# A 24th of the attention's exponentials as a polynomial on VectorE and GpSimd, and the wide exponential in two parts

## The chip, the cores and the metric

The kernel runs on one core of a Trainium2 chip. The metric is device time in microseconds (us). Before the change the median of three runs is 2979.16 us (2979.04 to 2981.36). Engines are named as the profile names them: PE is TensorE, PEld its weight loads, ACT is ScalarE, DVE is VectorE, POOL is GpSimd, and SP issues most DMAs.

## What is computed

A state-space convolution layer and an attention layer with one key and value head alternate, each twice, on a sequence of 2048 positions by 640 channels. All data is float32. The change touches the attention alone; the reference there, cut to what matters (the layer norm in front and the addition of the input behind are left out):

```
B, S, D = x.shape                    # 1, 2048, 640
H, Dh = 32, 20
q = (x @ wq).reshape(B, S, H, Dh).transpose(0, 2, 1, 3)
k = x @ wk                           # one head of 20 for all 32
v = x @ wv
scores = einsum("bhqd,bkd->bhqk", q, k) * (Dh ** -0.5)
p = softmax(scores)
o = einsum("bhqk,bkd->bhqd", p, v)
return o.transpose(0, 2, 1, 3).reshape(B, S, H * Dh) @ wo
```

The exponentials of the softmax are 32 x 2048 x 2048 in each of the two attention layers. No row maximum is searched in the usual case: a bound is put into two extra rows of the keys, so that the scores are ready for the exponential as they come out of the product.

## The kernel before

The program generates the convolution's kernel, runs convolution layer "a", attention layer "b", convolution layer "c" and attention layer "d". The loop that the change touches is `main_loop`, run once by each attention layer. It goes over 1024 tiles. A tile is 128 keys by 1024 columns: four heads by 256 queries. Its index i counts, from the inside, 16 blocks of keys (t), two halves of a query block (f), eight groups of four heads (hg) and four query blocks (nb). A tile takes three steps:

- `scores(i)` (line 1298): two matrix products into a PSUM tile `sc` of 128 x 1024. PSUM has three buffers of this size (`ps2`), taken in turn, so the scores of a tile wait until the tile three places earlier has been read.
- The exponential. Four tiles of six go the `direct` way: ACT reads `sc` and writes `pt` in SBUF (line 1304). The other two of six, those with i % 6 of 0 and 1, go `aside`: DVE copies `sc` into one half of an SBUF tile `pw` of 128 x 2048 (line 1311), and ACT later takes the exponential of both halves with one instruction of 2048 columns, in place (line 1429).
- `values(i)` (line 1321): four matrix products, one for each head, that add the tile's 128 keys into `po` in PSUM. They read four blocks of 256 columns of `pt` or `pw`.

After 32 tiles `normalize` moves `po` to SBUF and divides by the sums (DVE, lines 1336 to 1352), and SP writes the result into `ot`. `projection` (line 1393) multiplies a piece of `ot` by `wo` and `add` (line 1380, DVE) adds it to `x`. The projections are handed out by a credit, 0.52 for each half of an iteration and at most one per half, so that they lie between the scores and the values.

The order on PE, ACT and DVE is written out by hand (`manual_schedule`). One iteration c stands for six tiles:

```
w = wide.pop(c // 6, None)
if w is not None:
    nc.scalar.activation(flat(w), flat(w), AF.Exp, scale=SCALE)
for h in range(2):
    burst = [(c + 2 + 2 * h, direct), (c + 7 + 5 * h, aside), (c + 3 + 2 * h, direct)]
    for i, put in burst:
        if i < n:
            put(i, scores(i))
    ...
    behind([i for i in range(c - 3 + 3 * h, c + 3 * h) if 0 <= i < n])
```

So ACT runs the wide exponential of tiles c and c + 1, then four direct ones (c + 2 to c + 5). PE runs three scores, three values and perhaps a projection, twice. An aside tile is copied up to two iterations before its wide exponential. There are 171 iterations per layer and 170 wide exponentials. POOL has no arithmetic in the loop: it clears two small tiles, issues loads of weights at iteration 36 (`late_loads`) and a few stores of the result.

Of the kernel before, what the change touches and what calls it, by code (L numbers as in the profile page):

```python
# [11 lines left out]
F32 = mybir.dt.float32  # L12
F32R = mybir.dt.float32r
BF16 = mybir.dt.bfloat16
I32 = mybir.dt.int32
AF = mybir.ActivationFunctionType
ALU = mybir.AluOpType
# [4 lines left out]
P = 128  # L22
# [13 lines left out]
SCALE = 20.0**-0.5  # L36
LIMIT = 32.0 * 20.0**0.5
SAFE = ((LIMIT - 1e-6) / 1.002) ** 2


def channel_order():
# [154 lines left out]
class Net:  # L196
# [894 lines left out]
    def _attn(self, ctx, nm, out):  # L1091
# [19 lines left out]
        with tc.tile_pool(name=f"pj{nm}", bufs=1, reuse_waits="tile") as pj:  # L1111
# [116 lines left out]
            nc.scalar.activation(bnd[:, 1:2], bnd[:, 0:1], AF.Sqrt)  # L1228
            nc.vector.tensor_scalar(flag, bnd[0:1, 0:1], SAFE, None, ALU.is_le)
            nc.vector.tensor_scalar(bnd[:, 3:4], bnd[:, 0:1], SAFE, -1.0, ALU.is_le, ALU.mult)  # L1230

# [30 lines left out]
    def main_loop(self, ap, mp, kt, vt, nm, out):  # L1262
# [10 lines left out]
        tc, nc, qps = self.tc, self.nc, self.qps  # L1273
# [5 lines left out]
        def late_loads(late):  # L1279
            nc.gpsimd.memset(wol, 0.0)  # L1280
            for j in range(4):
                nc.gpsimd.dma_start(wol[32 * j : 32 * j + 20],
                                    self.ins["B_wo"][20 * (28 + j) : 20 * (29 + j)])
            if out is None:
                self.conv_weights(nc.gpsimd, late)

        tiles = [(nb, hg, f, t) for nb in range(4) for hg in range(8) for f in range(2) for t in range(16)]
        pos, pts, ots, wide = {}, {}, {}, {}
        queue, later = [], []

        def scores(i):
            nb, hg, f, t = tiles[i]
            if (nb, hg) not in qps:
                self.load_q(ap, nm, nb, hg)
            sc = self.ps2(f"sc{nm}{i}")
            for par in range(2):
                rows = slice(64 * par, 64 * par + 62)
                nc.tensor.matmul(sc[:, 512 * par : 512 * par + 512], kt[rows, 128 * t : 128 * t + 128],  # L1298
                                 qps[nb, hg][rows, f].rearrange("p a c -> p (a c)"), start=True, stop=True)
            return sc  # L1300

        def direct(i, sc):
            pts[i] = mp.tile([P, 1024], F32, tag="pt", bufs=5, name=f"pt{i}")
            nc.scalar.activation(pts[i], sc, AF.Exp, scale=SCALE)  # L1304

        def aside(i, sc):

            if i // 6 not in wide:
                wide[i // 6] = mp.tile([P, 2, 1024], F32, tag="pw", bufs=3, name=f"pw{i // 6}")
            pts[i] = wide[i // 6][:, i % 6]  # L1310
            nc.vector.tensor_copy(pts[i], sc)  # L1311

        def values(i):
            nb, hg, f, t = tiles[i]
            if (nb, hg) not in pos:
                pos[nb, hg] = self.ps1(f"po{nm}{nb}{hg}", hg % 2)
            po, pt = pos[nb, hg], pts.pop(i)

            for j in range(4):
                c0 = 512 * (j % 2) + 256 * (j // 2)  # L1320
                nc.tensor.matmul(po[32 * j : 32 * j + 32, 256 * f : 256 * f + 256], vt[:, t],  # L1321
                                 pt[:, c0 : c0 + 256], start=(t == 0), stop=(t == 15))

        def chunk(nb, k):
            if (nb, k) not in ots:
# [15 lines left out]
        def flat(a):  # L1341
            return a.rearrange("p a b -> p (a b)")
# [22 lines left out]
        def normalize_last():  # L1365

            po = pos.pop((3, 7))
            inv, steps = inverses(po, "l")
            for call in steps:
                call()  # L1370
            on = mp.tile([P, 512], F32, tag="on", bufs=2, name="onl")
            nc.vector.tensor_tensor(on, po, inv, ALU.mult)
            return on

        def add(nb, u, py, last):

            i, half = u // 2, u % 2
            t = TAUS[4 * nb + i]
            xh = self.x[:, t, 320 * half : 320 * half + 320]
            nc.vector.tensor_tensor(xh, py, xh, ALU.add)  # L1380
            if not last or half == 0:
                return
            if out is None:
                self.stats(t)
            else:
                for jh, eng in enumerate((nc.sync, nc.gpsimd if nb < 3 else nc.scalar)):
                    eng.dma_start(self.rows(out)[jh][:, t], self.x[64 * jh : 64 * jh + 64, t])

        def product(py, o, w, u, m, start, stop, c0=0, n=320):
            i, half = u // 2, u % 2  # L1390
            c0 += 320 * half
            for j in range(0, P, m):
                nc.tensor.matmul(py[j : j + m], o[:, 128 * i + j : 128 * i + j + m], w[:, c0 : c0 + n],  # L1393
                                 start=start, stop=stop)
# [8 lines left out]
        n = len(tiles)  # L1403
        credit, pieces = [0.0], []

        def behind(group):

            for i in group:
                values(i)
                if i % 32 == 31 and i + 1 < n:  # L1410
                    normalize(*tiles[i][:2])
            if not group:
                return
            if group[-1] % 32 >= (15 if group[-1] < n - 32 else 8):
                queue.extend(later)
                later.clear()
            credit[0] = min(credit[0] + 0.52, 1.5)
            if queue and credit[0] >= 1 and group[-1] % 32 not in (0, 1):
                credit[0] -= 1
                projection(tiles[group[-1]][1])  # L1420

        with tc.manual_schedule(engines={mybir.EngineType.PE, mybir.EngineType.Activation,
                                         mybir.EngineType.DVE}):
            for i, put in ((0, direct), (6, aside), (1, direct)):
                put(i, scores(i))
            for c in range(0, n, 6):
                w = wide.pop(c // 6, None)
                if w is not None:
                    nc.scalar.activation(flat(w), flat(w), AF.Exp, scale=SCALE)  # L1429
                for h in range(2):  # L1430
                    burst = [(c + 2 + 2 * h, direct), (c + 7 + 5 * h, aside), (c + 3 + 2 * h, direct)]
                    for i, put in burst:
                        if i < n:
                            put(i, scores(i))
                    if pieces:
                        pieces.pop(0)()
                    if c == 36 and h == 0:
                        late_loads(pts[38])
                    behind([i for i in range(c - 3 + 3 * h, c + 3 * h) if 0 <= i < n])
            behind([n - 1])  # L1440
            on = normalize_last()
            if out is None:
                self.norm("c", 0)

            last = []
            for g in range(3):
                tile_ = self.ps2(f"pl{nm}{g}")
                last += [tile_[:, 0:320], tile_[:, 512:832]]
            last.append(self.ps1(f"pl{nm}6", 0)[:, 0:320])
            last.append(self.ps1(f"pl{nm}7", 1)[:, 0:320])  # L1450
            left = queue + later
            for u in range(8):
                items = [(ots[nb, k], wo[:, k]) for nb, k, v in left if v == u and k < 4]
                items.append((ots[3, 4], wo[:, 4]))
                for n, (o, w) in enumerate(items):
                    product(last[u], o, w, u, P, n == 0, False)
            for u in range(0, 8, 2):
                for v in (u, u + 1):
                    product(last[v], on, wol, v, P, False, True)
                for v in (u, u + 1):  # L1460
                    add(3, v, last[v], True)
# [83 lines left out]
```

## Time and profile before

| What | Value |
|---|---|
| Median of three runs | 2979.16 us |
| The profiled execution: its time, its span | 2978.3 us, 2976.4 us |
| PE busy | 2733.0 us, 92% of the span |
| ACT busy | 2414.1 us, 81% |
| DVE busy | 2027.1 us, 68% |
| POOL busy | 84.9 us, 3% |
| Loop of layer "b", window 735 to 1664 us | ACT 923.66 and PE 908.62 of 929.00 us busy |
| Loop of layer "d", window 2030 to 2957 us | ACT 922.26 and PE 908.94 of 927.00 us busy |
| PE clock granted in both loops | 1.00 |

The page's span runs from the first to the last instruction; what lies outside it is 1.9 us. In the groups of the profile the first number is the busy time of the whole group in us and the second the mean duration of one in ns. Instructions of one engine can overlap in these records (the next starts while the last one writes its end), so on a busy engine the distance from start to start is the price of an instruction, and the duration is what another engine waits for. A row of the timeline merges neighbours of one kind ("x4"): its second number is then from the first start to the last end.

### The profile page before, as it was taken

The numbers are of one execution on the slowest core, as the hardware profiler recorded it, in microseconds if no ns is written. First come the engines' busy times: TensorE is split into PE (matmuls) and PEld (weight loads), VectorE is DVE, ScalarE is ACT, GpSimd is POOL, SyncE is SP. The second block draws the span as 40 slices with busy tenths as digits, with TensorE's granted clock in tenths as the row PEclk, the third lists the DMA queues.
The fourth block names the chain that finished last, engine by engine and source line by source line (L and its number), as shares of the span: only waits on it lengthen the run. The fifth ranks groups of instructions, "written<-read, shape, count | busy, mean of one in ns | idle before, by whom it ended". The sixth has DMA issues, their size and how long they took to land. (4 is left out here: it accounts for less than half of the span.)

```text
span 2976.4 us, 69802 instructions
## 1 busy us (share of the span) xinstructions
PE 2733.0 (92%) x29940; PEld 1570.6 (53%) x29940; DVE 2027.1 (68%) x2486; ACT 2414.1 (81%) x2565; POOL 84.9 (3%) x140
## 2 busy tenths in 40 slices
PE   2776989898999999999999998998999999999999
PEld 0333978775444444444444687774444444444444
DVE  7999899943566666666666699725566656666655
ACT  5888243454999999999999734338999999999997
POOL 0000001100000000000000011000000000000000
PEclk9655999998999999999999999999999999999999
DMA  6114555533200010101010256231001101110100
GB/s 146 34 17 103 183 167 114 139 104 104 82 23 27 22 26 22 28 21 28 23 27 20 88 114 161 65 128 43 22 27 31 35 23 32 35 28 23 44 20 24
DMA packets 144184, 178.81 MB, mean 60 GB/s; under 512 B 59524, under 2 KB 115844, under 8 KB 140244
## 3 DMA queue, kind: packets, MB, share of 16 engines
q1 hardware_dynamic: 119704, 141.90, 16.2%
q0 software_dynamic: 21872, 30.69, 5.6%
q8 instruction: 239, 3.92, 0.6%
q10 hardware_dynamic: 2288, 1.64, 0.2%
q14 instruction: 81, 0.66, 0.1%
HBM read 95.22 MB, written 48.04 MB: 48 GB/s over the span
## 5 line engine op out<-in xcount | busy, mean ns | idle before, releaser
L1304 ACT ACTIVATE pt<-scb 128x1024 f32<-128x1024 f32 x684 | 653.5, 1046 | 14.3 <-PE scb L1298 7.2
L1304 ACT ACTIVATE pt<-scd 128x1024 f32<-128x1024 f32 x684 | 652.5, 1044 | 12.7 <-PE scd L1298 7.2
L1429 ACT ACTIVATE pw<-pw 128x2048 f32<-128x2048 f32 x340 | 657.3, 1933 | 0.0
L1311 DVE COPY pw<-scd 128x1024 f32<-128x1024 f32 x340 | 415.4, 1222 | 218.1 <-PE scd L1298 215.0
L1311 DVE COPY pw<-scb 128x1024 f32<-128x1024 f32 x340 | 414.8, 1220 | 212.4 <-PE scb L1298 206.9
L1298 PE MATMUL scb<-qpb,kt 62*128 62x512 f32 x2048 | 378.6, 449 | 27.1 <-ACT pt L1304 17.7
L1298 PE MATMUL scd<-qpd,kt 62*128 62x512 f32 x2048 | 379.5, 449 | 24.4 <-ACT pt L1304 15.7
L1321 PE MATMUL pob<-pt,vt 128*32 128x256 f32 x5472 | 363.4, 383 | 0.1
L1321 PE MATMUL pod<-pt,vt 128*32 128x256 f32 x5472 | 362.9, 383 | 0.1
L1298 PEld LDWEIGHTS scb<-qpb,kt 62*128 62x128 f32 x2048 | 170.4, 186 | 260.9 <-ACT pt L1304 163.7
L1298 PEld LDWEIGHTS scd<-qpd,kt 62*128 62x128 f32 x2048 | 170.0, 185 | 259.7 <-ACT pt L1304 163.8
L1321 PEld LDWEIGHTS pob<-pt,vt 128*32 128x32 f32 x5472 | 160.6, 110 | 152.0 <-issue 63.9
L1321 PEld LDWEIGHTS pod<-pt,vt 128*32 128x32 f32 x5472 | 160.5, 110 | 152.0 <-issue 63.9
L1321 PE MATMUL pod<-pw,vt 128*32 128x256 f32 x2720 | 182.0, 385 | 1.0 <-DVE x L1380 1.0
L1321 PE MATMUL pob<-pw,vt 128*32 128x256 f32 x2720 | 182.0, 385 | 1.0 <-DVE x L1380 1.0
L1380 DVE TENSOR_TENSOR x<-pyd,x 128x320 f32<-128x320 f32 x149 | 72.6, 487 | 144.0 <-PE pyd L1393 144.0
L1380 DVE TENSOR_TENSOR x<-pyb,x 128x320 f32<-128x320 f32 x149 | 72.7, 488 | 141.0 <-PE pyb L1393 141.0
L1321 PEld LDWEIGHTS pob<-pw,vt 128*32 128x32 f32 x2720 | 71.1, 109 | 74.1 <-issue 42.4
L1321 PEld LDWEIGHTS pod<-pw,vt 128*32 128x32 f32 x2720 | 71.1, 109 | 73.3 <-issue 41.6
L1393 PE MATMUL pyb<-wo,ot 128*32 128x320 f32 x1192 | 107.5, 432 | 0.5 <-DMA ot<-on 0.5
L1393 PE MATMUL pyd<-wo,ot 128*32 128x320 f32 x1192 | 107.5, 432 | 0.4 <-DMA ot<-on 0.4
L654 PE MATMUL zc<-xnc,wf 128*128 128x256 f32 x384 | 87.4, 391 | 4.6 <-ACT xnc L821 4.5
(378 smaller groups left out, 3559.4 us busy)
## 6 DMA issues: line engine op xcount, KB each, us to landing
Akh<-kh SPq DMA_DIRECT2D x10, 2048.0 KB
kh<-Ak SPq DMA_DIRECT2D x5, 2048.0 KB
qhd<-qh SPq DMA_DIRECT2D x40, 256.0 KB
qld<-ql SPq DMA_DIRECT2D x40, 256.0 KB
qpb<-qhd SPq DMA_DIRECT2D x256, 40.0 KB
qpd<-qhd SPq DMA_DIRECT2D x256, 40.0 KB
ot<-on SPq DMA_DIRECT2D x216, 40.0 KB
wi<-in_c_wi SPq DMA_DIRECT2D x16, 512.0 KB
```

The source lines that it names most:

```text
L654: nc.tensor.matmul(zv[:, :, c, kk], self.wf[:, t + 4 * h, j, c, kk], x, start=(n == 0), stop=(n == 3))
L1298: nc.tensor.matmul(sc[:, 512 * par : 512 * par + 512], kt[rows, 128 * t : 128 * t + 128], qps[nb, hg][rows, f].rearrange("p a c -> p (a c) ...
L1304: nc.scalar.activation(pts[i], sc, AF.Exp, scale=SCALE)
L1311: nc.vector.tensor_copy(pts[i], sc)
L1321: nc.tensor.matmul(po[32 * j : 32 * j + 32, 256 * f : 256 * f + 256], vt[:, t], pt[:, c0 : c0 + 256], start=(t == 0), stop=(t == 15))
L1380: nc.vector.tensor_tensor(xh, py, xh, ALU.add)
L1393: nc.tensor.matmul(py[j : j + m], o[:, 128 * i + j : 128 * i + j + m], w[:, c0 : c0 + n], start=start, stop=stop)
L1429: nc.scalar.activation(flat(w), flat(w), AF.Exp, scale=SCALE)
```

## The change

Of the six tiles of an iteration the one with i % 6 = 0 loses its last 256 columns to a polynomial; that is 256 of 6144 columns. DVE copies only 768 columns of it to `pw`, which shrinks to 1792 columns. From the other 256, still in PSUM, DVE makes z, the score times SCALE / ln 2 times 2^23 as a whole number (line 1333 of the changed kernel). The lower 23 bits of z with the exponent of 1.0 give a float `zm` in [1, 2), the upper ones a power of two `ze` (lines 1334 and 1335). The first step of a polynomial of degree 5 in `zm` is made on DVE (1337); then POOL runs four pairs of `tensor_scalar` (multiply and add, line 1340) and `tensor_tensor` (multiply, 1341), the last pair with `ze`. The result `zh` is what `values` reads as fourth block.

The wide exponential is cut into 1280 columns, at its old place, and 512, between the direct exponentials of the first and the second half. `values` takes its blocks in the order 0, 2, 1, 3, so that the 512 columns of the later part are read last. POOL joins the engines whose order is written out.

```
+LOG2 = SCALE / math.log(2.0) * 2.0**23
+LOWEST = -125.0 * math.log(2.0) / SCALE
+POW2 = [0.4982859142799133, 0.35375531624817236, 0.10783493672886799, 0.03864472440553453,
+        -0.00039854327235786966, 0.0018775766733993503]
...
+        def blocks(a):
+            return [a[:, c0 : c0 + 256] for c0 in (0, 512, 256, 768)[: a.shape[1] // 256]]
+
         def direct(i, sc):
-            pts[i] = mp.tile([P, 1024], F32, tag="pt", bufs=5, name=f"pt{i}")
-            nc.scalar.activation(pts[i], sc, AF.Exp, scale=SCALE)
+            pt = mp.tile([P, 1024], F32, tag="pt", bufs=5, name=f"pt{i}")
+            nc.scalar.activation(pt, sc, AF.Exp, scale=SCALE)
+            pts[i] = blocks(pt)

         def aside(i, sc):
-            if i // 6 not in wide:
-                wide[i // 6] = mp.tile([P, 2, 1024], F32, tag="pw", bufs=3, name=f"pw{i // 6}")
-            pts[i] = wide[i // 6][:, i % 6]
-            nc.vector.tensor_copy(pts[i], sc)
+            n, h = i // 6, i % 6
+            if n not in wide:
+                wide[n] = mp.tile([P, 1792], F32, tag="pw", bufs=3, name=f"pw{n}")
+            if h == 1:
+                nc.vector.tensor_copy(wide[n][:, 768:], sc)
+                pts[i] = blocks(wide[n][:, 768:])
+                return
+            nc.vector.tensor_copy(wide[n][:, :768], sc[:, :768])
+            w = wide[n]
+            pts[i] = [w[:, 0:256], w[:, 512:768], w[:, 256:512], power(i, sc[:, 768:])]
+
+        def power(i, sc):
+            z, m, e = (mp.tile([P, 256], I32, tag=t, bufs=b, name=f"{t}{i}")
+                       for t, b in (("z", 1), ("zm", 2), ("ze", 2)))
+            h = mp.tile([P, 256], F32, tag="zh", bufs=3, name=f"zh{i}")
+            c = POW2
+            nc.vector.tensor_scalar(z, sc, LOWEST, LOG2, ALU.max, ALU.mult)
+            nc.vector.tensor_scalar(m, z, 0x7FFFFF, 0x3F800000, ALU.bitwise_and, ALU.bitwise_or)
+            nc.vector.tensor_scalar(e, z, 0x7F800000, 0x40000000, ALU.bitwise_and, ALU.bitwise_xor)
+            m, e = m.bitcast(F32), e.bitcast(F32)
+            nc.vector.scalar_tensor_tensor(h, m, c[4] / c[5], m, op0=ALU.add, op1=ALU.mult)
+            for a, b, f in ((0.5 * c[5], 0.5 * c[3], m), (1.0, 0.5 * c[2], m), (1.0, 0.5 * c[1], m),
+                            (1.0, 0.5 * c[0], e)):
+                nc.gpsimd.tensor_scalar(h, h, a, b, ALU.mult, ALU.add)
+                nc.gpsimd.tensor_tensor(h, h, f, ALU.mult)
+            return h
...
-            for j in range(4):
-                c0 = 512 * (j % 2) + 256 * (j // 2)
-                nc.tensor.matmul(po[32 * j : 32 * j + 32, 256 * f : 256 * f + 256], vt[:, t],
-                                 pt[:, c0 : c0 + 256], start=(t == 0), stop=(t == 15))
+            for j in (0, 2, 1, 3):
+                nc.tensor.matmul(po[32 * j : 32 * j + 32, 256 * f : 256 * f + 256], vt[:, t], pt[j],
+                                 start=(t == 0), stop=(t == 15))
...
         with tc.manual_schedule(engines={mybir.EngineType.PE, mybir.EngineType.Activation,
-                                         mybir.EngineType.DVE}):
+                                         mybir.EngineType.DVE, mybir.EngineType.Pool}):
...
-                if w is not None:
-                    nc.scalar.activation(flat(w), flat(w), AF.Exp, scale=SCALE)
                 for h in range(2):
+                    if w is not None:
+                        cols = w[:, 1280 * h : 1280 + 512 * h]
+                        nc.scalar.activation(cols, cols, AF.Exp, scale=SCALE)
```

What stands on ACT for iteration c = 240 of layer "b", before (`pw40` is its wide tile, `pt242` to `pt245` are its direct ones):

```order
L1429 ACTIVATE pw40_13207<-pw40_13207 128x2048 [waits DVE_49]
L1304 ACTIVATE pt242_13291<-scb242_13288 128x1024 [waits PE_49,Activation_49]
L1304 ACTIVATE pt243_13300<-scb243_13297 128x1024 [waits PE_49,Activation_49]
L1304 ACTIVATE pt244_13323<-scb244_13320 128x1024 [waits PE_49,Activation_49]
L1304 ACTIVATE pt245_13333<-scb245_13330 128x1024 [waits PE_49,Activation_49]
```

and in the changed kernel:

```order
L1461 ACTIVATE pw40_13869<-pw40_13869 128x1280 [waits DVE_49]
L1311 ACTIVATE pt242_13986<-scb242_13983 128x1024 [waits PE_49,Activation_49]
L1311 ACTIVATE pt243_13995<-scb243_13992 128x1024 [waits PE_49,Activation_49]
L1461 ACTIVATE pw40_13869<-pw40_13869 128x512
L1311 ACTIVATE pt244_14019<-scb244_14016 128x1024 [waits PE_49,Activation_49]
L1311 ACTIVATE pt245_14045<-scb245_14042 128x1024 [waits PE_49,Activation_49]
```

ACT has one instruction more and 256 columns fewer, and the second part stands between the two pairs.

On DVE at the same place of layer "b" (tiles 246, 247, 252 and 253 are the aside ones of the next two wide tiles; line 1380 is `add`), before:

```order
L1311 COPY pw41_13268<-scb246_13265 128x1024 [waits PE_49,Activation_49]
L1311 COPY pw41_13268<-scb247_13293 128x1024 [waits PE_49]
L1380 TENSOR_TENSOR x_66<-pyb030_13314,x_66 128x320 [waits PE_49]
L1311 COPY pw42_13328<-scb252_13325 128x1024 [waits PE_49,Activation_49]
L1380 TENSOR_TENSOR x_66<-pyb031_13347,x_66 128x320 [waits PE_49]
L1311 COPY pw42_13328<-scb253_13359 128x1024 [waits PE_49]
```

and in the changed kernel:

```order
L1323 COPY pw41_13947<-scb246_13944 128x768 [waits PE_49,Activation_49]
L1333 TENSOR_SCALAR z246_13949<-scb246_13944 128x256 [waits DVE_49]
L1334 TENSOR_SCALAR zm246_13950<-z246_13949 128x256 [waits DVE_49,Pool_49]
L1335 TENSOR_SCALAR ze246_13951<-z246_13949 128x256 [waits Pool_49]
L1337 SCALAR_TENSOR_TENSOR zh246_13952<-zm246_13950 128x256 [waits DVE_49]
L1320 COPY pw41_13947<-scb247_13988 128x1024 [waits PE_49]
L1410 TENSOR_TENSOR x_66<-pyb030_14009,x_66 128x320 [waits PE_49]
L1323 COPY pw42_14024<-scb252_14021 128x768 [waits PE_49,Activation_49]
L1333 TENSOR_SCALAR z252_14026<-scb252_14021 128x256 [waits DVE_49]
L1334 TENSOR_SCALAR zm252_14027<-z252_14026 128x256 [waits DVE_49,Pool_49]
L1335 TENSOR_SCALAR ze252_14028<-z252_14026 128x256 [waits Pool_49]
L1337 SCALAR_TENSOR_TENSOR zh252_14029<-zm252_14027 128x256 [waits DVE_49]
```

Behind every second aside copy stand four more instructions; the PSUM tile is released after the second of the five.

POOL has nothing at this place before. In the changed kernel one tile's share is:

```order
L1340 TENSOR_SCALAR zh246_13952<-zh246_13952 128x256 [waits DVE_49,PE_49]
L1341 TENSOR_TENSOR zh246_13952<-zh246_13952,zm246_13950 128x256 [waits Pool_49]
L1340 TENSOR_SCALAR zh246_13952<-zh246_13952 128x256 [waits Pool_49]
L1341 TENSOR_TENSOR zh246_13952<-zh246_13952,zm246_13950 128x256 [waits Pool_49]
L1340 TENSOR_SCALAR zh246_13952<-zh246_13952 128x256 [waits Pool_49]
L1341 TENSOR_TENSOR zh246_13952<-zh246_13952,zm246_13950 128x256 [waits Pool_49]
L1340 TENSOR_SCALAR zh246_13952<-zh246_13952 128x256 [waits Pool_49]
L1341 TENSOR_TENSOR zh246_13952<-zh246_13952,ze246_13951 128x256 [waits Pool_49]
```

Each of the eight waits for the one ahead of it to have landed.

More of the change, by code (lines that the diff above doesn't have):

```diff
@@ L1437, in main_loop @@
                     if c == 36 and h == 0:
-                        late_loads(pts[38])
+                        late_loads(pts[38][0])
                     behind([i for i in range(c - 3 + 3 * h, c + 3 * h) if 0 <= i < n])
```

## The prediction, made before the changed kernel had run

> **What bounds the kernel now.** I read the page's busy shares first, then the windows of the two loops, then the timeline of ACT and PE inside one of them. The windows (us of the stretch, then busy us of PE, PEld, DVE, ACT, POOL):
>
> ```profile
> 735.00:1664.00 929.00, 908.62 (x11290) 433.02 (x11294) 575.48 (x673) 923.66 (x843) 5.69 (x17) 1.00 0.10 28
> 2030.00:2957.00 927.00, 908.94 (x11286) 432.55 (x11282) 564.99 (x637) 922.26 (x842) 6.90 (x13) 1.00 0.10 27
> ```
>
> The loops are 1856 of 2976 us. ACT is busy for 99.4% of them and PE for 98%, so busy shares don't tell which one sets the pace; the starts do. The timeline of ACT gives the first and the last wide exponential of each loop, and one iteration between:
>
> ```profile
> 729.26 1.91 ACT L1429 ACTIVATE pw<-pw 128x2048 f32<-128x2048 f32 x1
> 1661.88 1.91 ACT L1429 ACTIVATE pw<-pw 128x2048 f32<-128x2048 f32 x1
> 2024.62 1.91 ACT L1429 ACTIVATE pw<-pw 128x2048 f32<-128x2048 f32 x1
> 2955.74 1.91 ACT L1429 ACTIVATE pw<-pw 128x2048 f32<-128x2048 f32 x1
> ...
> 2030.04 1.94 ACT L1429 ACTIVATE pw<-pw 128x2048 f32<-128x2048 f32 x1
> 2031.84 3.80 ACT L1304 ACTIVATE pt<-scd 128x1024 f32<-128x1024 f32 x4
> 2035.45 1.98 ACT L1429 ACTIVATE pw<-pw 128x2048 f32<-128x2048 f32 x1
> ```
>
> With 169 intervals between the first and the last of 170, an iteration takes 932.62/169 = 5.518 us in layer "b" and 931.12/169 = 5.510 in "d", 5.514 on average. Without a wait ACT needs 1.80 for the wide exponential (2030.04 to 2031.84) and 3.61 for the four direct ones, together 5.41. So ACT sets the pace, and 0.10 us of each iteration are slips.
>
> PE follows closely. Its rows in an iteration with one projection, none of them marked with a wait:
>
> ```profile
> 1011.02 0.97 PE L1298 MATMUL scb<-qpb,kt 62*128 62x512 f32 x6
> 1011.91 1.50 PE L1321 MATMUL pob<-pt,vt 128*32 128x256 f32 x24
> 1013.35 1.07 PE L1298 MATMUL scb<-qpb,kt 62*128 62x512 f32 x6
> 1014.35 1.07 PE L1321 MATMUL pob<-pw,vt 128*32 128x256 f32 x16
> 1015.24 0.61 PE L1321 MATMUL pob<-pt,vt 128*32 128x256 f32 x8
> 1015.67 0.72 PE L1393 MATMUL pyb<-wo,ot 128*32 128x320 f32 x8
> 1016.32 0.97 PE L1298 MATMUL scb<-qpb,kt 62*128 62x512 f32 x6
> ```
>
> From score to score that is 5.30 us. The projection takes 0.65 of it (1015.67 to 1016.32); without one, values to scores take 1.44 (1011.91 to 1013.35) in place of 1.32 (1014.35 to 1015.67), so PE needs 5.30 - 0.65 + 0.12 = 4.77. The rows of DVE below count 298 projections in 342 iterations, 0.87 each: PE's mean is 5.30 - 0.13 x 0.53 = 5.23. **The room between ACT's 5.41 and PE is 0.1 to 0.2 us.**
>
> **The change, ACT.** The wide instruction becomes one of 1280 and one of 512 columns. The price of an SBUF source by size comes from the 1.80 above and from an exponential-sized instruction of 1024 columns elsewhere:
>
> ```profile
> 70.68 1.04 ACT L436 ACTIVATE s<-f 128x1024 f32<-128x1024 f32 x1
> 71.62 1.13 ACT L437 ACTIVATE c<-fa,halfpi 128x1024 f32<-128x1024 f32 x1
> ```
>
> 0.94 from start to start for 1024, 1.80 for 2048: 0.84 ns a column and 0.08 us for the instruction. So 1280 cost 1.16, 512 cost 0.51, together 1.67 in place of 1.80. The 256 columns taken away are worth 0.21, and the second instruction gives 0.08 back. ACT's floor goes from 5.41 to **5.28**.
>
> The place of the second part helps PE. The scores of c + 5 wait for the PSUM tile that the direct exponential of c + 3 reads; the wide part between the pairs puts 0.51 between that release and the time at which ACT wants c + 5. I count on the slips of today going away for that reason, but with PE at 5.30 in most iterations the pace is then PE's: 5.31, and 0.02 more because the projections are not spread evenly (a guess).
>
> **DVE.** Its groups in the loop:
>
> ```profile
> L1311 DVE COPY pw<-scd 128x1024 f32<-128x1024 f32 x340 | 415.4, 1222 | 218.1 <-PE scd L1298 215.0 <-ACT pt L1304 0.2
> L1311 DVE COPY pw<-scb 128x1024 f32<-128x1024 f32 x340 | 414.8, 1220 | 212.4 <-PE scb L1298 206.9 <-ACT pt L1304 1.2
> L1380 DVE TENSOR_TENSOR x<-pyb,x 128x320 f32<-128x320 f32 x149 | 72.7, 488 | 141.0 <-PE pyb L1393 141.0
> L1380 DVE TENSOR_TENSOR x<-pyd,x 128x320 f32<-128x320 f32 x149 | 72.6, 487 | 144.0 <-PE pyd L1393 144.0
> L1336 DVE STREAM_TRANSPOSE tr<-on 128x512 f32<-128x512 f32 x62 | 44.1, 712 | 2.1
> L1352 DVE TENSOR_TENSOR on<-on,tr 128x512 f32<-128x512 f32 x62 | 42.3, 682 | 0.0
> L1347 DVE COPY on<-pod 128x512 f32<-128x512 f32 x31 | 21.3, 689 | 7.9 <-PE pod L1321 6.3 <-DMA qpd<-qhd 1.4 <-DMA qpd<-qld 0.2
> ...
> L117 DVE SCALAR_TENSOR_TENSOR Aa<-B x36: 681/686/693, 407.6 to 566.7; 128x512 f32<-128x512 f32 x36
> L281 DVE TENSOR_SCALAR th<-thr x1: 493/493/493, 10.2 to 10.2; 128x640 f32<-128x640 f32 x1
> ```
>
> A copy out of PSUM takes 0.689 for 512 and 1.22 for 1024 columns: 0.96 for 768 and 0.42 for 256. So the shorter copy saves 0.26, and z costs 0.42. The two bit operations go from SBUF to SBUF; the nearest row, 0.493 for 640 columns, gives 0.29 each (the 0.155 that remain of a copy at no columns, and half its price per column). The first step of the polynomial reads two SBUF operands like L117: 0.42. Together DVE gets -0.26 + 0.42 + 0.29 + 0.29 + 0.42 = 1.16 us more per iteration. It is busy for 575.48 of 929, 62% of 5.51 = 3.42; then 4.58 of 5.33, 86%. What hides this is the time in which DVE waits for scores, 215.0 + 206.9 us or 1.24 per iteration, and for projections, 285 us or 0.84. The PSUM tile is free after copy and z, 1.4 us in place of 1.22, and the next aside scores come 2.6 later. The three instructions behind them stand ahead of the next copy: 1.4 + 1.06 (with the small gaps between) = 2.5 fits in 2.6, with an `add` or a piece of `normalize` (0.49 to 0.71) it doesn't, and the next copy is late. It has about an iteration until its tile is wanted, so most of it is absorbed; I charge 0.05.
>
> **POOL.** The trace has no arithmetic of POOL on more than one element. The nearest rows:
>
> ```profile
> L1280 POOL MEMSET wol<- 128x640 f32 x2 | 1.3, 636 | 233.9 <-PEq L1249 233.9
> L427 POOL MEMSET c<- 128x32 f32 x20 | 3.1, 156 | 187.0 <-DVE e1r L464 141.7 <-DVE resare L261 37.4 <-ACT m L453 7.9
> L592 POOL COPY wf<-pt 1x1 f32<-1x1 f32 x8 | 1.0, 173 | 38.6 <-ACT pt L1304 38.6
> L1527 POOL MEMSET const-float32-0.0<- 128x1 f32 x1 | 0.1, 98 | 0.2 <-issue 0.2
> 598.12 2.79 POOL L1103 MEMSET kt<- 1x1536 f32 x2
> L1103 POOL MEMSET kt<- x4: 1367/1370/1372, 598.1 to 1895.3; 1x1536 f32 x4
> 718.93 2.12 POOL L1282 DMA_DIRECT2D wol<-in_B_wo  x4 [0.30 <-POOL wol L1280]
> 760.56 4.21 POOL L598 DMA_DIRECT2D wf<-in_c_wf  x8
> ```
>
> Writing costs (0.636 - 0.156)/608 = 0.79 ns a column, so 0.33 for 256 columns; reading adds 0.075 at one element (0.173 against 0.098); an instruction that waits for the one ahead on POOL starts 0.05 behind it (two of 1.37 in 2.79). **Low end:** reading is free, eight of 0.33 with eight gaps: 3.1 us. **High end:** every operand is a pass of its own (0.20 each): 0.61 for the `tensor_scalar`, 0.81 for the `tensor_tensor`, chain 6.1. **I take** reading of one operand beside the writing and the second operand as a pass: 0.41 and 0.61, chain 4 x 1.02 + 0.4 = 4.5. The result is wanted two iterations later, so the latency is covered; only the throughput counts, 4.5 of 5.3. The GPSIMD Engine Reference of the Trainium skill (section 3.1) measures 4497 ns for a `tensor_tensor` of 2048 columns and puts one-input operations near line rate; as an estimate that is 0.56 to 0.62 for 256 columns and a chain near 4.3. No run here shows it yet.
>
> Once in layer "b", at iteration 36, clearing and loading the weights (0.64 + 2.12 + 1.00 + 4.21 = 8.0 us of POOL) stand in POOL's order ahead of the polynomial; I charge 1 us.
>
> **The sum.** 5.31 + 0.02 + 0.05 = 5.38 against 5.514, so 0.134 x 340 = 46 us less, 1 us back: 2978.3 (the profiled execution: span 2976.4 and 1.9 around it) - 45 = 2933. The median of the runs is 0.9 above that execution: **2934 us**.
>
> **Rivals.** *POOL's chain sets the pace (slower).* Values of each aside tile with i % 6 = 0 wait for `zh`. It decides from the point at which the eight take over 5.51, 0.63 each with the gap taken off. At the high end, 6.1, the loop is 0.6 x 340 = 204 us longer: 3182. For it speaks that POOL goes from 3% to 85% on operations that no row prices; against it that the MEMSETs lie at half that price.
>
> *POOL and DVE shut each other out.* The two bit operations run at half a price per column, which L281 against a copy shows, and the fourth operation reads two SBUF operands; should DVE use for this a way into SBUF that POOL needs too, then 1.06 us of DVE and the chain can't overlap except in the chain's gaps: 4.5 + 1.06 = 5.56 down to 5.16. With the upper price the loop is 0.05 x 340 = 17 us longer, 2995; in the middle nothing changes, 2980. The Trainium skill's page "SBUF — State Buffer" (section "Who interferes with whom") says just that: such DVE instructions and a POOL instruction hold a shared port pair, and the second to issue blocks fully. The trace of before cannot show it, since POOL was idle in the loop.
>
> *PE keeps the pace near today's.* The slips stay at 0.10 and come on top of PE's 5.30 in most iterations and 5.28 in the rest: 5.45 with the 0.05 of DVE, 22 us less, 2956.
>
> *The split does nothing* because 0.08 per instruction is too low: at 0.21 it would eat the gain. ACT's rows at two sizes exclude that.
>
> **Chances.** The forecast 0.40 (2902 to 2955); PE near today's pace 0.15 (2950 to 2972); POOL and DVE shut out 0.25, of which 0.12 within 0.2% and 0.13 slower (to 3040); POOL's chain 0.20 (2986 to 3182). Faster by over 0.2%, which is about what a measurement of this kernel can tell from no change, 0.55; within it 0.12; slower 0.33. The lower end of the range is ACT's floor without any slip, (5.514 - 5.29) x 340 = 76 us less; the upper end, 3075, takes in the port's case and half of the chain's.
>
> **What would show it.** ACT: starts 1.16 and 0.51 apart behind the two parts; iterations of 5.38 by the first and the last start. DVE: the bit operations at 0.29, and longer ones if POOL shuts them out. POOL: about 4.5 busy per iteration, mean of the two operations near 0.41 and 0.61; PE without waits for `zh`. I am wrong if POOL is busy all the time, if PE waits for POOL or for DVE's copies, or if ACT now waits for scores as long as it has gained.

## The result, and the profile after

| | median, us | range of the runs, us | against before, 95% interval |
|---|---|---|---|
| before | 2980.26 | 2979.04 to 2981.56 (4) | |
| predicted | 2934 | 2902 to 3075 | |
| after | 3004.32 | 3002.54 to 3005.79 (4) | 1.0080 (1.0063 to 1.0098) |

The changed kernel is 24 us slower; 46 us faster was forecast. The first and the last start of the wide exponential's first part, in each of the two loops:

```profile
731.15 1.26 ACT L1461 ACTIVATE pw<-pw 128x1280 f32<-128x1280 f32 x1
1676.10 1.31 ACT L1461 ACTIVATE pw<-pw 128x1280 f32<-128x1280 f32 x1
2038.93 1.26 ACT L1461 ACTIVATE pw<-pw 128x1280 f32<-128x1280 f32 x1
2982.49 1.31 ACT L1461 ACTIVATE pw<-pw 128x1280 f32<-128x1280 f32 x1
```

Over 169 intervals each that is 5.591 and 5.583 us an iteration, 5.587 on average, against 5.514 before and 5.38 forecast: 0.073 x 340 = 25 us, so the loss lies in the loops. The windows of the same two stretches as before (us, then busy us of PE, PEld, DVE, ACT and POOL):

```profile
735.00:1664.00 929.00, 897.21 (x11128) 445.44 (x11128) 778.07 (x1333) 897.74 (x998) 813.03 (x1352) 0.99 0.10 28
2030.00:2957.00 927.00, 906.70 (x11097) 448.41 (x11101) 768.83 (x1295) 900.03 (x996) 809.11 (x1342) 0.99 0.11 29
```

ACT and PE have both lost share; DVE has gone from 62% to 84% and POOL from 1% to 88%. That DVE and POOL are busy doesn't say which of them is waited for. The groups of the polynomial do (busy us of the group, mean ns of one, idle us ahead of them):

```profile
L1341 POOL TENSOR_TENSOR zh<-zh,zm 128x256 f32<-128x256 f32 x1020 | 784.5, 769 | 85.1
L1341 POOL TENSOR_TENSOR zh<-zh,ze 128x256 f32<-128x256 f32 x340 | 256.5, 754 | 28.3
L1340 POOL TENSOR_SCALAR zh<-zh 128x256 f32<-128x256 f32 x1360 | 602.0, 443 | 372.1 <-DMA qpd<-mxd 123.8 <-ACT pt L1311 123.7 <-DVE zh L1337 7.0
L1337 DVE SCALAR_TENSOR_TENSOR zh<-zm 128x256 f32<-128x256 f32 x340 | 205.8, 605 | 0.0
L1334 DVE TENSOR_SCALAR zm<-z 128x256 int32<-128x256 int32 x340 | 146.1, 430 | 36.8 <-POOL zh L1340 0.9 <-POOL zh L1341 0.5 <-DVE z L1333 0.5
L1335 DVE TENSOR_SCALAR ze<-z 128x256 int32<-128x256 int32 x340 | 133.9, 394 | 0.0
```

POOL is hardly ever idle for want of work: 7.0 us in all on DVE's `zh`. The two waits of 124 us lie ahead of the first chain of each loop; of the rest, the idle time ahead of a `tensor_tensor` is 113.4 us for 1360, 0.083 each, which is the gap behind the instruction that it depends on, and ahead of a `tensor_scalar` it is about the same (117.6 us for 1360). Four pairs then take 4 x (0.765 + 0.443) + 8 x 0.084 = 5.50 us, and what POOL does besides (8.3 us for the loads of layer "b", about 9 us for loads and stores in "d") is another 0.05 to 0.06; that brings the time from one chain to the next to 5.56, close to the 5.587 of the iteration. **POOL has nearly no time without work in the loops, so it sets the pace.**

How POOL and DVE slow each other is seen in their timelines (start, duration), first POOL's:

```profile
1000.75 0.76 POOL L1341 TENSOR_TENSOR zh<-zh,zm 128x256 f32<-128x256 f32 x1
1001.60 0.66 POOL L1340 TENSOR_SCALAR zh<-zh 128x256 f32<-128x256 f32 x1
...
1003.17 0.41 POOL L1340 TENSOR_SCALAR zh<-zh 128x256 f32<-128x256 f32 x1
1003.65 0.73 POOL L1341 TENSOR_TENSOR zh<-zh,ze 128x256 f32<-128x256 f32 x1
1004.47 0.40 POOL L1340 TENSOR_SCALAR zh<-zh 128x256 f32<-128x256 f32 x1
```

and DVE's in the same microseconds:

```profile
1000.83 0.83 DVE L1335 TENSOR_SCALAR ze<-z 128x256 int32<-128x256 int32 x1
1001.59 0.41 DVE L1337 SCALAR_TENSOR_TENSOR zh<-zm 128x256 f32<-128x256 f32 x1
```

The bit operation at 1000.83 begins inside a POOL instruction that lasts until 1001.51 and takes 0.83 us; without POOL it is 0.29 (e3_no_pool, below). It ends at 1001.66 and the fused instruction behind it at 1002.00. POOL's `tensor_scalar` at 1001.60 starts beside them and takes 0.66; the undisturbed one at 1003.17 takes 0.41. Each engine pays for the other.

The same rows show which of the two holds up the chains. DVE has finished its part of a tile at 1002.00, and POOL begins with that tile at 1004.47, behind the chain that ends at 1004.38. Worked out in this way from both timelines, between 740 and 1640 us and between 2040 and 2900, POOL begins a chain 2.5 us (layer "b") and 3.3 us ("d") after DVE has finished its part, as a median, and in only 5 of 316 chains less than 0.2 after it. DVE's stretched instructions are done long before POOL wants their result.

What became late, from the waits over the whole execution (us in total, times, longest):

```profile
ACT pt L1311 <- PE scb L1302: 34.8, 58, 4.7
...
PEld scb L1302 <- DVE pw L1320: 24.3, 32, 1.8
PEld pod L1351 <- POOL zh L1341: 21.5, 49, 0.9
...
PEld pob L1351 <- POOL zh L1341: 11.5, 28, 1.5
```

PE waits 77 times (49 and 28) for `zh` itself, and for copies that DVE makes late; ACT in turn waits for scores.

### The profile page after: what moved, and what is told of

It is laid out like the page before. It is cut to its first block, busy times and chain, and to the rows that moved or that the text cites. A ratio compares the mean times of both kernels' runs of the same rounds, so it can differ in the third digit from the quotient of the medians.

```text
span 3004.0 us, 75220 instructions
## 1 busy us (share of the span) xinstructions
PE 2744.7 (91%) x29940; PEld 1609.3 (54%) x29940; DVE 2451.6 (82%) x3846; ACT 2389.5 (80%) x2905; POOL 1728.2 (58%) x2860
## 5 line engine op out<-in xcount | busy, mean ns | idle before, releaser
L1341 POOL TENSOR_TENSOR zh<-zh,zm 128x256 f32<-128x256 f32 x1020 | 784.5, 769 | 85.1
L1340 POOL TENSOR_SCALAR zh<-zh 128x256 f32<-128x256 f32 x1360 | 602.0, 443 | 372.1 <-DMA qpd<-mxd 123.8
L1461 ACT ACTIVATE pw<-pw 128x1280 f32<-128x1280 f32 (+1 forms) x680 | 669.3, 984 | 0.0
L1341 POOL TENSOR_TENSOR zh<-zh,ze 128x256 f32<-128x256 f32 x340 | 256.5, 754 | 28.3
L1323 DVE COPY pw<-scd 128x768 f32<-128x768 f32 x170 | 161.8, 952 | 92.0 <-PE scd L1302 78.4
L1323 DVE COPY pw<-scb 128x768 f32<-128x768 f32 x170 | 161.6, 951 | 86.0 <-PE scb L1302 67.5
L1320 DVE COPY pw<-scb 128x1024 f32<-128x1024 f32 x170 | 205.9, 1211 | 16.3 <-PE scb L1302 15.2
L1320 DVE COPY pw<-scd 128x1024 f32<-128x1024 f32 x170 | 206.5, 1215 | 14.3 <-PE scd L1302 13.0
L1337 DVE SCALAR_TENSOR_TENSOR zh<-zm 128x256 f32<-128x256 f32 x340 | 205.8, 605 | 0.0
L1334 DVE TENSOR_SCALAR zm<-z 128x256 int32<-128x256 int32 x340 | 146.1, 430 | 36.8 <-POOL zh L1340 0.9
```

Of the source, the lines that this page charges most:

```text
L1320: nc.vector.tensor_copy(wide[n][:, 768:], sc)
L1323: nc.vector.tensor_copy(wide[n][:, :768], sc[:, :768])
L1334: nc.vector.tensor_scalar(m, z, 0x7FFFFF, 0x3F800000, ALU.bitwise_and, ALU.bitwise_or)
L1337: nc.vector.scalar_tensor_tensor(h, m, c[4] / c[5], m, op0=ALU.add, op1=ALU.mult)
L1340: nc.gpsimd.tensor_scalar(h, h, a, b, ALU.mult, ALU.add)
L1341: nc.gpsimd.tensor_tensor(h, h, f, ALU.mult)
```

## The experiments

"Iteration" is worked out as above, from the first and the last start in each loop, as a mean of the two loops. "POOL's need" is the pairs by the kernel's own means plus 0.084 a gap.

| label | median, us | against before, 95% interval | iteration, us | POOL's need, us |
|---|---|---|---|---|
| e1_split_only | 2993.28 | 1.0045 (1.0028 to 1.0061) | 5.548 | 0 |
| e2_three_pairs | 2933.54 | 0.9843 (0.9827 to 0.9860) | 5.374 | 3.99 |
| e3_no_pool | 2935.68 | 0.9850 (0.9834 to 0.9867) | 5.377 | 0 |
| e4_transposes | 2947.89 | 0.9892 (0.9875 to 0.9908) | 5.418 | 5.30 |
| e6_unsplit | 2950.48 | 0.9902 (0.9886 to 0.9919) | 5.432 | 4.00 |
| e7_z_only | 2926.88 | 0.9821 (0.9805 to 0.9838) | 5.359 | 0 |
| e8_five_pairs | 3434.39 | 1.1523 (1.1504 to 1.1542) | 6.825 | 6.79 |
| e9_cut_1024 | 2933.52 | 0.9840 (0.9824 to 0.9857) | 5.375 | 3.99 |
| e10_deferred | 2936.17 | 0.9853 (0.9837 to 0.9870) | 5.385 | 3.98 |
| e11_bits_kept | 2968.91 | 0.9962 (0.9948 to 0.9976) | 5.483 | 5.40 |
| e12_stt_kept | 2972.02 | 0.9970 (0.9960 to 0.9981) | 5.487 | 5.40 |

The theory after the result: POOL's chain sets the pace, because its instructions are dearer than forecast and because DVE's added instructions shut it out of SBUF. The rivals: DVE's load, by copies that come late, or the split and the new order.

### The chain shorter, gone, and longer

**e2_three_pairs**: degree 4 with coefficients of its own, so one pair less.

```
-POW2 = [0.4982859142799133, 0.35375531624817236, 0.10783493672886799, 0.03864472440553453,
-        -0.00039854327235786966, 0.0018775766733993503]
+POW2 = [0.50996419, 0.31201612, 0.16661329, -0.00212517, 0.01353416]
...
-nc.vector.scalar_tensor_tensor(h, m, c[4] / c[5], m, op0=ALU.add, op1=ALU.mult)
-for a, b, f in ((0.5 * c[5], 0.5 * c[3], m), (1.0, 0.5 * c[2], m), (1.0, 0.5 * c[1], m),
-                (1.0, 0.5 * c[0], e)):
+nc.vector.scalar_tensor_tensor(h, m, c[3] / c[4], m, op0=ALU.add, op1=ALU.mult)
+for a, b, f in ((0.5 * c[4], 0.5 * c[2], m), (1.0, 0.5 * c[1], m), (1.0, 0.5 * c[0], e)):
```

> A polynomial of one degree less: three pairs of tensor_scalar and tensor_tensor on POOL in place of four; all DVE and ACT work stays. Unhindered chain by the changed kernel's trace: 3 x (0.405 + 0.731) + 6 x 0.084 = 3.91 us, with DVE's interference at most 4.2. Theory (POOL's chain sets the pace): POOL has over 1 us to spare in each iteration, pace falls to PE's and ACT's, 5.33 to 5.42, 2918 to 2948 us, faster than before. Rival (DVE's added load, late copies): DVE's work is unchanged, so 5.5 to 5.6 stays, 2975 to 3005 us. Rival (contention of the two engines for SBUF costs DVE the time): most of it stays, since three quarters of POOL's instructions stay, over 2965 us.

**e3_no_pool**: the loop over the pairs is left out.

> All eight POOL instructions of the polynomial are left out (the values read what DVE's first step of the polynomial left, so those exponentials are not computed); DVE's four added instructions stay. Theory (POOL's chain sets the pace): 5.31 to 5.40 us an iteration, 2911 to 2941 us, with the bit operations at 0.28 to 0.32 and the fourth DVE operation near 0.40, no longer stretched. Rival (DVE's load sets the pace): 5.5 to 5.6 stays, 2975 to 3005 us.

**e8_five_pairs**: one pair more.

```
-                (1.0, 0.5 * c[0], e)):
+                (1.0, 0.5 * c[0], m), (1.0, 0.0, e)):
```

> A fifth pair on POOL (one more multiplication by the same factor, so those exponentials are not the reference's); the rest is the changed kernel's. Theory (POOL's chain sets the pace): unhindered chain 5 x (0.405 + 0.731) + 10 x 0.084 = 6.52 us, and 0.08 to the next, 0.08 of POOL's other work, and 0.1 to 0.3 from DVE's interference: 6.78 to 6.98 an iteration, 3410 to 3480 us; POOL's waits then rule PE and ACT. Rival (the chain is only one of several limits and POOL's queue is partly hidden): well under 6.5 an iteration, below 3320 us.

All three fell where the theory had them, and none where a rival had it. With DVE's work unchanged, one pair less takes 71 us away, and taking away the other three gives nothing more (2933.5 and 2935.7). A pair more costs 430 us, 1.24 an iteration, about what a pair needs. The timeline of POOL in e2_three_pairs shows the spare time that the changed kernel lacks, a wait for DVE between two chains:

```profile
1003.25 0.41 POOL L1338 TENSOR_SCALAR zh<-zh 128x256 f32<-128x256 f32 x1
1003.74 0.73 POOL L1339 TENSOR_TENSOR zh<-zh,ze 128x256 f32<-128x256 f32 x1
1005.88 0.41 POOL L1338 TENSOR_SCALAR zh<-zh 128x256 f32<-128x256 f32 x1 [1.41 <-DVE zh L1336]
```

POOL here begins a chain 0.16 us after DVE's part, as a median, and so the two engines seldom work at the same time: DVE's three instructions take 309, 287 and 423 ns in this run, nearly as without POOL. e2_three_pairs and e3_no_pool therefore take away both the full chain and the stretching; how much each is worth is seen only in the next group of runs.

In e8_five_pairs the wait for `zh` stands openly in PE's waits, 333 times for 340 chains in place of 77:

```profile
PEld pod L1351 <- POOL zh L1341: 259.8, 167, 4.8
PEld pob L1351 <- POOL zh L1341: 253.3, 166, 4.4
```

The prices of DVE's added instructions without a busy POOL are in the groups of e3_no_pool:

```profile
L1337 DVE SCALAR_TENSOR_TENSOR zh<-zm 128x256 f32<-128x256 f32 x340 | 142.3, 419 | 0.0
L1334 DVE TENSOR_SCALAR zm<-z 128x256 int32<-128x256 int32 x340 | 100.0, 294 | 11.6
L1335 DVE TENSOR_SCALAR ze<-z 128x256 int32<-128x256 int32 x340 | 97.4, 286 | 0.0
```

Beside POOL's four pairs they take 605, 430 and 394: 0.43 us more an iteration together.

### DVE and POOL shutting each other out

**e4_transposes**: the three DVE instructions that work from SBUF to SBUF become transposes; z, m and e are float tiles for this, and z is scaled by SCALE in place of LOG2.

```
-nc.vector.tensor_scalar(m, z, 0x7FFFFF, 0x3F800000, ALU.bitwise_and, ALU.bitwise_or)
-nc.vector.tensor_scalar(e, z, 0x7F800000, 0x40000000, ALU.bitwise_and, ALU.bitwise_xor)
-nc.vector.scalar_tensor_tensor(h, m, c[4] / c[5], m, op0=ALU.add, op1=ALU.mult)
+nc.vector.transpose(m, z)
+nc.vector.transpose(e, z)
+nc.vector.transpose(h, m)
```

> POOL keeps its eight instructions, and DVE keeps its load, but the two bit operations and the fused add and multiply are replaced by three transposes of 128x256 (so those exponentials are not computed), a kind of DVE instruction whose duration the changed kernel's trace shows the same beside a busy POOL (0.712 for 512 columns). Theory in its fine part (the chain is 5.22 unhindered and is stretched by 0.29 by DVE instructions that shut POOL out of SBUF): POOL's pairs fall to 0.405 and 0.731, the chain to 5.22 to 5.28, the iteration to 5.33 to 5.45, 2918 to 2958 us; POOL then is still nearly always busy. Rival (no shutting out; POOL's instructions are that slow by themselves or by any DVE work): chain 5.4 to 5.5 and iteration 5.55 to 5.6 stay, 2992 to 3009 us.

**e11_bits_kept** takes the last line of this diff alone, **e12_stt_kept** the first two with the float tiles.

> The changed kernel with the fused add and multiply alone replaced by a transpose of 128x256 (so those exponentials are not the reference's); the two bit operations and POOL's eight instructions stay. Replacing all three was worth 56 us (3004 to 2948). Theory (each of the three shuts POOL out, by about the same amount): about a third of it, 2977 to 2993 us; the bit operations still have a mean well over 0.29 us. Rival (only the instruction with two SBUF operands shuts POOL out): 2944 to 2954. Rival (only the bit operations do): 3000 to 3008.

> The changed kernel with the two bit operations alone replaced by transposes of 128x256 (so those exponentials are not computed); the fused add and multiply, with its two SBUF operands, and POOL's eight instructions stay. Theory (each of the three shuts POOL out, by about the same amount): two thirds of the 56 us come back, 2959 to 2975 us; the fused instruction still has a mean well over 0.42 us. Rival (only the instruction with two SBUF operands shuts POOL out): 3000 to 3008. Rival (only the bit operations do): 2944 to 2954.

In e4_transposes DVE is loaded as before (its three take 1.25 in place of 1.43 stretched and 1.00 alone), and POOL does all its work; yet it is 56 us faster. Its groups:

```profile
L1340 POOL TENSOR_TENSOR zh<-zh,zm 128x256 f32<-128x256 f32 x1020 | 757.6, 743 | 85.1
L1339 POOL TENSOR_SCALAR zh<-zh 128x256 f32<-128x256 f32 x1360 | 563.4, 414 | 386.0 <-DVE zh L1336 137.8 <-DMA qpd<-mxd 124.3 <-DVE rc L1366 3.3
L1334 DVE STREAM_TRANSPOSE zm<-z 128x256 f32<-128x256 f32 x340 | 151.4, 445 | 38.7 <-POOL zh L1340 2.4 <-DVE z L1333 0.9 <-POOL zh L1339 0.5
L1335 DVE STREAM_TRANSPOSE ze<-z 128x256 f32<-128x256 f32 x340 | 136.8, 402 | 0.9 <-POOL zh L1340 0.9
```

POOL's pair falls from 1.208 to 1.156 us and its need from 5.50 to 5.30, just above the 5.22 to 5.28 that were expected. In layer "d" the iteration is 5.386, which is 0.197 less than the changed kernel's 5.583: about what POOL's need has lost. In "b" it is 5.450 against 5.591, since POOL there also waits, 17 times and 12.6 us in all, for DVE or PE. So the shutting out costs 0.17 an iteration on average, 57 us, and without it POOL's need and its other instructions come to the pace of the kernels without a chain (5.377).

The Trainium skill's page "SBUF — State Buffer", section "Who interferes with whom", says that a DVE instruction with two inputs in SBUF, and a `tensor_scalar` in a mode with two ports, share a port pair with POOL as an exclusive lock. The two half experiments agree that both kinds are stretched beside POOL; whether one engine is blocked fully they don't show. Replacing the fused instruction is worth 35 us and replacing the bit operations 32 us; the kind that stays is still stretched (the groups of e11_bits_kept, then of e12_stt_kept):

```profile
L1334 DVE TENSOR_SCALAR zm<-z 128x256 int32<-128x256 int32 x340 | 151.7, 446 | 36.8 <-DVE z L1333 1.4 <-POOL zh L1340 0.5
L1335 DVE TENSOR_SCALAR ze<-z 128x256 int32<-128x256 int32 x340 | 131.3, 386 | 0.0
```

```profile
L1336 DVE SCALAR_TENSOR_TENSOR zh<-zm 128x256 f32<-128x256 f32 x340 | 203.7, 599 | 0.0
```

e12_stt_kept fell in its band; e11_bits_kept came out 8 us below it, so my equal thirds were wrong: the one fused instruction costs more than half as much as the three. POOL's need falls by 0.10 in each run, and the two halves do add up to the 0.20 of e4_transposes; the times don't (35 + 32 against 56), probably since in e4_transposes POOL also waits in layer "b". In both half runs POOL's need of 5.40 and 0.08 make the iteration. What no edit separates: these runs take away DVE's own stretching too. That POOL in the changed kernel begins its chains 2.5 to 3.3 us after DVE's part speaks for POOL's stretching as the one that decides.

### The split and the order

**e1_split_only**: no polynomial, `pw` of 2048 columns, cut into 1536 and 512.

```
...
-cols = w[:, 1280 * h : 1280 + 512 * h]
+cols = w[:, 1536 * h : 1536 + 512 * h]
```

> The split and its place alone: no polynomial, the wide buffer holds two whole tiles again (2048 columns), split into 1536 and 512, the 512 still between two pairs of direct exponentials; POOL does no arithmetic in the loop. ACT's floor is 0.08 + 0.84 x 1.536 = 1.37, plus 0.51, plus 3.61 = 5.49 us an iteration, against 5.41 before. Theory (POOL's chain sets the pace of the changed kernel): without the chain ACT is the bound and the place of the second part takes the slips away, 5.49 to 5.54 an iteration, 2972 to 2989 us. Rival (the split and the new order themselves cost the time, by scores or copies that come late): the changed kernel's 5.59 or more stays, 3005 us or more.

**e6_unsplit**: e2_three_pairs with the wide exponential in one.

```
+if w is not None:
+    nc.scalar.activation(w, w, AF.Exp, scale=SCALE)
 for h in range(2):
-    if w is not None:
-        cols = w[:, 1280 * h : 1280 + 512 * h]
-        nc.scalar.activation(cols, cols, AF.Exp, scale=SCALE)
```

> Three pairs on POOL as in e2_three_pairs, but the wide exponential of 1792 columns is one instruction again, ahead of both pairs of direct ones. By ACT's rows (5.41 an iteration with 2048 columns in one, 0.215 for 256 columns) its floor is 5.20 us in place of the 5.295 that most iterations of e2_three_pairs show. Theory (the prediction's: PE needs 5.30 and the place of the second part keeps PE fed): without the place the slips of before, 0.10, come on top of PE's pace, 5.39 to 5.42 an iteration, 2937 to 2949 us. Rival (the second part's instruction, 0.10 by e1_split_only, is pure cost): 5.28 to 5.35, 2900 to 2925 us.

**e9_cut_1024**: e2_three_pairs with the cut elsewhere.

```
-cols = w[:, 1280 * h : 1280 + 512 * h]
+cols = w[:, 1024 * h : 1024 + 768 * h]
```

> e2_three_pairs with the wide exponential cut at 1024 in place of 1280: 1024 columns first, 768 between the pairs. ACT's floor stays (two instructions, 1792 columns): 5.295. Theory (what counts is that something of ACT's stands between the pairs, and 512 columns are enough): the same time as e2_three_pairs within 6 us, 2927 to 2940. Rival (the longer the part between the pairs, the better PE is fed): 5.32 to 5.35 an iteration, 2914 to 2925 us.

The split and the new order alone are slower than before, by 13 us; the time lies between the two bands of the expectation. ACT's timeline there:

```profile
1304.21 1.97 ACT L1460 ACTIVATE pw<-pw 128x1536 f32<-128x1536 f32 x1
1305.59 2.42 ACT L1311 ACTIVATE pt<-scb 128x1024 f32<-128x1024 f32 x2
1307.39 1.13 ACT L1460 ACTIVATE pw<-pw 128x512 f32<-128x512 f32 x1
1307.91 2.43 ACT L1311 ACTIVATE pt<-scb 128x1024 f32<-128x1024 f32 x2
1309.72 2.00 ACT L1460 ACTIVATE pw<-pw 128x1536 f32<-128x1536 f32 x1
```

From start to start 1.38, 1.80, 0.52 and 1.81: the floor is 5.51, so the second instruction costs 0.10 over the 5.41 of before, and 0.04 of slips are left of 0.10. Most of the slips do go, but the 0.06 gained is less than the 0.10 that the second instruction costs. Once the polynomial has made ACT shorter, it is the other way round. ACT's timeline in e6_unsplit:

```profile
1309.10 1.74 ACT L1457 ACTIVATE pw<-pw 128x1792 f32<-128x1792 f32 x1
1310.68 3.81 ACT L1310 ACTIVATE pt<-scb 128x1024 f32<-128x1024 f32 x4
1314.30 1.78 ACT L1457 ACTIVATE pw<-pw 128x1792 f32<-128x1792 f32 x1
```

Its floor is 5.20 and its mean 5.432, 0.23 above; e2_three_pairs has a floor of 5.29 and a mean of 5.374, 0.08 above. The second instruction costs 0.09 there and takes away 0.15 of slips, which is worth 17 us. The median of e6_unsplit lies 1.5 us above the theory's band and far from the rival's. That PE is fed better, as the prediction had argued, agrees with ACT's waits for scores, 41.9 us in e6_unsplit and 22.7 in e2_three_pairs. Whether the cut is at 1024 or 1280 makes no difference: e9_cut_1024 gives the same time.

### DVE's load

**e7_z_only**: e3_no_pool without DVE's two bit operations and fused instruction too; z is written as the result.

> As e3_no_pool, and of DVE's four added instructions only the first (the one that reads PSUM) is left; the two bit operations and the fused add and multiply are left out too (so those exponentials are not computed). DVE is relieved of 1.0 us per iteration against e3_no_pool. Theory (DVE's three further instructions cost the prediction's 0.05 by copies that come late): 5.375 falls to about 5.32, 2917 us, 2910 to 2922. Rival (they are covered entirely by DVE's waiting): 2931 to 2938, no change against e3_no_pool. Rival (late copies make up all that is over 5.295): 2905 to 2910.

**e10_deferred**: e2_three_pairs, in which these three and the chain are put behind the next copy.

```
 if h == 1:
     nc.vector.tensor_copy(wide[n][:, 768:], sc)
+    held.pop(0)()
...
 nc.vector.tensor_scalar(z, sc, LOWEST, LOG2, ALU.max, ALU.mult)
+held.append(lambda: rest(z, m, e, h))
+return h
```

> e2_three_pairs with DVE's two bit operations and its fused add and multiply (and so POOL's chain) put behind the next copy of 1024 columns in place of ahead of it; nothing else differs. e7_z_only has shown that leaving them out is worth 9 us (0.026 an iteration). Theory (they cost by making the 1024 copy late): half of the 9 us or more comes back, 2924 to 2930 us. Rival (now the copy of 768 columns is late in its place): 2931 to 2940 us.

1.0 us of DVE's work per iteration costs 9 us in all by the medians, 0.026 an iteration: half of the prediction's 0.05, between the bands of e7_z_only. Moving it behind the next copy brings none of it back, so the theory of e10_deferred failed, and the time is in its rival's band. That a late copy is what costs the 9 us is therefore not shown. What is left above ACT's 5.29 in e7_z_only, 0.07, was not traced further.

## Why the prediction was wrong, point by point

- **ACT: right.** 1.16 and 0.51 were forecast, with a floor of 5.28. In e2_three_pairs, whose ACT work is the changed kernel's, the starts are:

```profile
1299.65 1.49 ACT L1459 ACTIVATE pw<-pw 128x1280 f32<-128x1280 f32 x1
1300.81 2.15 ACT L1310 ACTIVATE pt<-scb 128x1024 f32<-128x1024 f32 x2
1302.62 0.86 ACT L1459 ACTIVATE pw<-pw 128x512 f32<-128x512 f32 x1
1303.13 2.17 ACT L1310 ACTIVATE pt<-scb 128x1024 f32<-128x1024 f32 x2
1304.94 1.52 ACT L1459 ACTIVATE pw<-pw 128x1280 f32<-128x1280 f32 x1
```

  1.16 and 0.51, as forecast, and 5.29 in all.
- **The pace without POOL's chain, 5.38: right as a sum, in part by luck.** It is the 5.374 and 5.377 of e2_three_pairs and e3_no_pool, and the 2934 us of the forecast are e2_three_pairs's 2933.5. But two errors cancel: without DVE's three instructions the pace was to be 5.31 + 0.02 = 5.33 and is 5.359 (e7_z_only), and the 0.05 for these three is 0.02 to 0.03. That PE sets this pace isn't shown either: in the rows above ACT starts without a wait, and between 735 and 1630 us of e2_three_pairs it is busy for 888.60 of 895.00 us, PE for 878.10.
- **DVE's own prices: right** (0.29, 0.29 and 0.42 forecast; 294, 286 and 419 ns in e3_no_pool), but only for a DVE that isn't shut out.
- **POOL's chain, "4.5 of 5.3": this step failed, and what was wrong is the size of the term.** The `tensor_scalar` was right: 0.41 forecast, 0.414 in e4_transposes. The `tensor_tensor` takes 0.743 there, not 0.61, and the gap is 0.084, not 0.05. Beside transposes, four pairs need 5.30, not 4.5. The value lies between the two ends that were worked out, nearer to the high one; I took the cheaper reading for the second operand. The estimate of 0.56 to 0.62 from the Trainium skill's page "GPSIMD Engine Reference" (section 3.1), which gives a time for 2048 columns, is low for 256 columns as well.
- **"Only the throughput counts, 4.5 of 5.3": the 0.8 us to spare failed with it.** At 5.30 there is no spare, and then every stretching of a POOL instruction is the iteration's.
- **The shutting out: the rival was right in kind and given too little (0.25).** Its upper sum, 4.5 + 1.06, stood on the wrong 4.5, and 1.06 was too much. POOL's need grows by 0.20 (from 5.30 to 5.50) and DVE's instructions by 0.43. That a part of DVE's operations falls in POOL's gaps would explain the difference, but isn't shown.
- **The sign hangs on both failures.** With POOL's real prices and the shutting out mostly gone the change is e4_transposes, 1.1% faster than before. With room in the chain the shutting out itself nearly goes away, and it is e2_three_pairs, 1.6% faster. In these runs only both together end on the other side.
- **The loads at iteration 36: 1 us was charged, 3 to 8 came.** Ahead of the loads POOL copies an element of one of ACT's `pt` tiles eight times. Behind a full POOL these copies are late, and ACT waits for the tile, in the changed kernel's timeline:

```profile
767.61 1.00 POOL L596 COPY wf<-pt 1x1 f32<-1x1 f32 x8
768.64 1.02 ACT L1311 ACTIVATE pt<-scb 128x1024 f32<-128x1024 f32 x1 [2.90 <-POOL wf L596]
```

  ACT's wait is 3 of 24 us. As POOL sets the pace, the 8.3 us that it spends here between two chains count against it too, 0.05 an iteration of layer "b". Either is a small part of the 70 us between forecast and result.
- **The place of the 512 columns: right with the polynomial** (e2_three_pairs against e6_unsplit: 0.15 of slips gone for 0.09), a loss without it (e1_split_only: 0.06 gone for 0.10).

The kernel that beats both is e2_three_pairs, or e9_cut_1024, which can't be told from it: one degree less, 1.6% faster than before.

## What to carry to other kernels

Before work goes to an idle engine, its throughput has to be priced with every operand and every gap between dependent instructions counted; an engine filled to 85% by estimate has no room for an estimate that is 18% off. Ask also what the engine beside it does in the meantime: between DVE and POOL the choice of the instruction (one from SBUF to SBUF with two operands, a `tensor_scalar` or a transpose) decided over 50 us here. Moving a part of an instruction to a better place pays only if the waits that it takes away are longer than the price of the additional instruction.

## What the runs showed of the hardware that was not expected

DVE's copies out of PSUM aren't stretched beside a full POOL, nor is its transpose of 512 columns. The copy of 768 columns takes 951 ns in the changed kernel and 952 in e3_no_pool, and the transpose of 512 columns 712 in both. The product of two SBUF tiles in `normalize` is stretched: 808 ns against 677. The rows, of the changed kernel and then of e3_no_pool:

```profile
L1323 DVE COPY pw<-scb 128x768 f32<-128x768 f32 x170 | 161.6, 951 | 86.0 <-PE scb L1302 67.5 <-ACT pw L1461 16.3 <-ACT pt L1311 1.4
L1382 DVE TENSOR_TENSOR on<-on,tr 128x512 f32<-128x512 f32 x62 | 50.1, 808 | 0.0
L1366 DVE STREAM_TRANSPOSE tr<-on 128x512 f32<-128x512 f32 x62 | 44.1, 712 | 2.1
```

```profile
L1323 DVE COPY pw<-scb 128x768 f32<-128x768 f32 x170 | 161.9, 952 | 102.1 <-PE scb L1302 86.4 <-ACT pw L1457 9.5 <-ACT pt L1311 4.8
L1378 DVE TENSOR_TENSOR on<-on,tr 128x512 f32<-128x512 f32 x62 | 42.0, 677 | 0.0
L1362 DVE STREAM_TRANSPOSE tr<-on 128x512 f32<-128x512 f32 x62 | 44.1, 712 | 2.1
```
